# One core, same instructions: another order of the turns of an attention and MLP kernel

## The chip, the core and the metric

The kernel runs on one core of a Trainium2 chip. The metric is the device time of one execution in microseconds (us). The core has a matrix engine (PE in the profile, with its weight loads as PEld), VectorE (DVE), ScalarE (ACT), GpSimd (POOL), and a queue that only issues transfers (SP). Each executes its own list of instructions in order; semaphores make one wait for another. So the order in which the program issues instructions is the order in which each engine must take them.

## The reference

```
state = alpha[:, :, t, :, None] * state + einsum('bhd,bhe->bhde', k[:, :, t], v[:, :, t])
y[:, :, t] = einsum('bhd,bhde->bhe', q[:, :, t], state)          # for each t
x  = y with the heads side by side                                # (4, 768, 384)
xn = (x - mean) / sqrt(var + 1e-6) * g_ln
out = x + maximum(xn @ w_ch1, 0) @ w_ch2                          # 384 -> 1536 -> 384
```

Four batches of 8 heads, 768 steps and 48 channels go through a gated recurrence; its result goes through a normalisation and a two-layer MLP with a residual. The two weight matrices arrive as 64-bit floats.

## The kernel before

The 768 steps are cut into 6 chunks of 128. A chunk of one batch is one unit of attention, so there are 24 units, named a to x (a to d are chunk 0, e to h chunk 1, and so on). Within a chunk the recurrence is done by matrix products: logarithms of the gates are summed by a triangular matrix (L317, L320, L407), q and k are scaled by the exponentials (ACT L324 and L325, DVE L327 and L329), transposed (on PE, L355, in chunks 0 and 1; later on DVE, L366, and through DRAM on SP's queue, L372 and L379), multiplied into scores (L397, L405), masked by DVE (L411, L417), and turned into the result (L458, or L463 and L467). The state is carried by L432 on PE, L445 on DVE and a gate product on POOL (L447). Each result is copied out of PSUM (L493, L481), normalised (L512 to L523) and transposed (L530, or L536 and DRAM).

The MLP of chunk 0 is computed plainly: hidden products L567 (turns Y and Z, one per half of the batches), relu L570, second layer L579 (P and Q), residual L583. Chunks 1 to 5 use a scheme with fewer products: instead of nine block products it takes 15 of the first layer's (L857, turns 1 and 2 for the two halves of the hidden units) and 20 of the second layer's (L683, turn M), of combined blocks. Combinations are made by DVE: of the first weights (S), of the second weights (W, L643), of x (X, L834), of the hidden values after the relu (N, L670). Results are put together by DVE from PSUM (L867 to L900, L693, L696), by ACT (copies L865, L873, L887, L702 to L743) and by late adds on POOL (L876 to L896, L699). R and U are the relus (ACT L907), O fetches the residual.

The weights are brought in twelve pieces, turns A to L (A to F the first matrix, G to L the second). Each piece is loaded into one of three staging buffers and rounded from 64 bits to 32 by three DVE instructions (L219, L221, L223), one on ACT (L227) and further ones on DVE (L229 with L233 or L236). The load of the piece three later is issued in the last turn.

Six PSUM banks are shared by all products (tag "bank"). A product can start only when a bank has been read out by its last reader.

Every unit is a Python generator; each yield ends one turn. The order of all turns is written out by hand as one string of 1508 letters, and a letter executes the next turn of its generator:

```
turns = {"YZ"[h]: first_of_chunk_0(h) for h in range(2)}
turns |= {"PQ"[h]: second_of_chunk_0(h) for h in range(2)}
turns |= {chr(ord("a") + n): attention(n // B, n % B) for n in range(NCB * B)}
turns |= {chr(ord("A") + i): take_weights(i) for i in range(len(pieces))}
turns |= {"M": mlp(), "S": combine_first(), "W": combine_weights(),
          "1": hidden_products(0), "2": hidden_products(1), "R": relus(0), "U": relus(1),
          "X": (x for c in range(1, NCB) for x in combine_x(c)),
          "N": (x for c in range(1, NCB) for x in combine_hidden(c)), "O": outputs()}
with tc.manual_schedule():
    for turn in ORDER:
        next(turns[turn], None)
```

"Turn 17 of i" below means the code of unit i between its 17th and 18th yield, counted from 0. A turn issues between none and eight or so instructions; the products of one unit's turn 17 are 64 small matmuls.

Of the kernel before, what the change touches and what calls it, by code (L numbers as in the profile page):

```python
# [30 lines left out]


ORDER = (
    "bacabcadaacbcaadbcadabcababbebaccbadbaaBbccaedcbceAeeaaacbfecfBcdafddeaedbdeafae"
    "bcdccbfgadhAdcgCcdbebeebfhggdfgbfffbCdcgfgecdfchgdfhgabcddchdhAiiegjhacehedhhjfg"
    "biAdfidAeBhBijffYYiCjZZYYifZYlZCgjYDlYYjjZZYBZYgDieEgDgDjZZekEhZYGZgZigZGeeYgYgg"
    "fZYEhfGfkChihiYFYijfgEhgkhFZYhgYfghijgkFeZZlGZShfZYHlhHfYFYZeZHelYiZgllPmZkJIgJk"
    "PeiYjJIflHeSZIQgkIlYSjiPkffennSQlOKjLSnSjmSQhKnSjLnKPkiljnhSQnLkkjkWknkShOmPhkhl"
    "kOOhWlmmphmQmkmXjWQnXjlSQjPmkilXSXkP2OXWjXQjkjW2iXoSWX2oWX22Pi2mnol1j1mom2omSpoo"
    "l1XSpk2oW2m112p1m2pm11m1W211pp12O122r22jnn21lpnmnjSml1riOn2l12Rl111kqS1m21W1Rkp2"  # L40
    "o21mUXpq1mU2rUrnmj1rl2Rno2oomqonrormpokO1rNM2Mipin1op1ionoqUM2qp2W12RkMmNqiMoRtk"
    "UrpkqNM1NoMliMlNUMMNMNMKNqMlNorMWrnmtltNRMsqppMWNMriMMMpNlsqqqnoqttNttMtMsXMMssM"
    "sMNMNMX1oXXppMvstM2MXMMNMsppXoMXoqMsMMXM1nqqv11Xq1trMq2tqX21rn12v1r2ur2r222rvsqs"
    "svsu1rs1nuvvt2s11ss11p22rtsvosn2uropuXru222221uts212stnU1211u1121222Op1Rp2tRU21R"
    "Us1pXqU11x2tO2MM1vwMUM12xuRvu1vurNNNNwtOuuMwRxvNtxRNutwwMM2MOwNXwMNuXMMtNM1rMMMw"
    "qtXMMMxNUNxtMMsNMMMxXxMtXtrMMqMNrMXNvutMMwNuMMMNMMMxMLMOM11vvuq2X2O2wMus1wX11222"
    "2r2Xt1222w22utsqxvw2x2ww1vx21sX12121xwvq2O2x2w111u1uvU121w12s1wuRvx12U11J1q21R1U"
    "OvRxU121wMMu2xxsRNMw2NNMRM1MUNN2MMuUMqXN1MrNNRMNvMXNXMMMM2MMMxNM1uNXMMNMNMOXMXMv"
    "MMXOMMMXxNxwxMMvNMMMMMXMx21w1x222212v12w222x122w2212X11UX2212121121121wx111MU11X"
    "2RR2v1211212211R1URU211XOUM2XNRX1MX1RM2MXN2MXNXNMXXMXMMMN111U1MN1M1122MNM1MM2MM1"  # L50
    "11NNN121O11NM1MM21N1112N1122M1MMM12MM12N222M22M2RM1M2N22MM2MU1ON2M22M2UURR22RNNM"
    "MNM1MMOMRMNMUUM2ONMNNNMO2MMMUMNMMMMMRMMNNMMMNMNMMNMMMMMMMMNMNMMMMMMM"
)


# [913 lines left out]
```

## Time and profile before

| | |
|---|---|
| time, median of 3 runs | 420.37 us (420.18 to 420.57) |
| the profiled execution's own time | 420.64 us |
| its span, first to last instruction | 418.9 us |
| granted PE clock | 1.00 |
| bytes moved by DMA | 59.52 MB, 142 GB/s on average |

The span is the part that the profile covers; the rest of the profiled execution's time, 1.7 us, lies around it. Busy shares are of the span. An idle engine is listed with the instruction that waited and the one that released it. The chain that ended last is followed back from the last instruction, at each step to what released it.

### The profile page before, as it was taken

What the parts mean: (1) busy time and instruction counts of PE and PEld (TensorE: products, weight loads), DVE (VectorE), ACT (ScalarE), POOL (GpSimd) and SP (SyncE); (2) the same over time, 40 slices, a digit from 0 to 9 for tenths busy, and PEclk for the clock granted to TensorE, in tenths of its full rate; (3) what the DMA queues carried; (4) which work ended last, traced back from release to release, by engine and by line L of the source; (5) the groups of instructions that cost most, each with busy time, mean ns of one, the idle gap of its engine ahead of it and who ended that gap; (6) DMA issues with size and microseconds to landing.
All of it is one profiled execution on the core that took longest, in us unless ns stands there. A gap on an engine that the chain in (4) does not pass through costs nothing.

```text
span 418.9 us, 11553 instructions
## 1 busy us (share of the span) xinstructions
PE 409.0 (98%) x4608; PEld 360.9 (86%) x4608; DVE 351.4 (84%) x713; ACT 178.0 (42%) x440; POOL 153.2 (37%) x169
## 2 busy tenths in 40 slices
PE   6998999999999999999999999999999999999996
PEld 4787888766678889998889999889998899999996
DVE  3999999999999989996888996688876767977873
ACT  5498456724243496414546612364313242014110
POOL 3011000003203990043395033493152940499123
PEclk9999999999999999999999999999999999999999
DMA  7998889987778778587784546433035200001201
GB/s 247 325 297 246 206 201 293 287 194 181 145 221 176 200 167 185 128 195 178 146 215 70 130 105 166 88 95 77 0 114 104 67 1 2 0 20 38 94 20 56
DMA packets 133741, 59.52 MB, mean 142 GB/s; under 512 B 90764, under 2 KB 129804, under 8 KB 133688
## 3 DMA queue, kind: packets, MB, share of 16 engines
q1 hardware_dynamic: 133688, 58.79, 55.1%
q8 instruction: 36, 0.59, 0.6%
q14 instruction: 17, 0.14, 0.1%
HBM read 42.17 MB, written 16.61 MB: 140 GB/s over the span
## 4 chain that ended last, share of the span: by engine, by line
PE 89%; DVE 4%; ACT 2%; DMA 2%; issue 1%; SPq 1%; POOL 0%; POOLq 0%; DVEq 0%
PE hps L857 31%; PE ops L683 30%; PE ops L579 8%; PE hps L567 8%; PE aps L405 3%; PE yps L463 3%; PE yps L467 2%; PE sums L432 2%; DMA rq<-in_q_dram 2%; PE xps L530 1%; PE tps L355 1%; PE aps L397 1%; PE lps L407 1%; SPq L132 1%; DVE w L221 0%
## 5 line engine op out<-in xcount | busy, mean ns | idle before, releaser
L699 POOL TENSOR_TENSOR ob<-ob,u 128x192 f32<-128x192 f32 x40 | 26.3, 668 | 64.5 <-DVE ob L696 48.3
L857 PE MATMUL hps<-sum,w 128*128 128x256 f32 x192 | 46.3, 381 | 0.0
L907 ACT ACTIVATE hT<-hT 128x512 f32<-128x512 f32 x48 | 28.8, 624 | 34.9 <-POOL hT L879 18.5
L447 POOL TENSOR_TENSOR mid<-mid,gate 112x192 f32<-112x192 f32 x20 | 11.4, 568 | 80.0 <-DVE mid L445 33.3
L683 PE MATMUL ops<-w,hT 128*128 128x192 f32 x224 | 40.5, 327 | 0.0
L857 PEld LDWEIGHTS hps<-sum,w 128*128 128x128 f32 x192 | 36.1, 190 | 5.0
L683 PEld LDWEIGHTS ops<-w,hT 128*128 128x128 f32 x224 | 37.1, 190 | 0.7 <-issue 0.2
L857 PE MATMUL hps<-xT,w 128*128 128x256 f32 x136 | 34.0, 380 | 0.0
L579 PE MATMUL ops<-w,hT 128*128 128x384 f32 x96 | 33.0, 491 | 0.0
L567 PE MATMUL hps<-xT,w 128*128 128x256 f32 x144 | 32.5, 382 | 0.0
L567 PEld LDWEIGHTS hps<-xT,w 128*128 128x128 f32 x144 | 27.0, 190 | 4.2
L683 PE MATMUL ops<-ws,sum 128*128 128x192 f32 x160 | 28.7, 327 | 0.0
L857 PEld LDWEIGHTS hps<-xT,w 128*128 128x128 f32 x136 | 25.5, 190 | 3.1
L683 PEld LDWEIGHTS ops<-ws,sum 128*128 128x128 f32 x160 | 26.5, 190 | 0.3
L579 PEld LDWEIGHTS ops<-w,hT 128*128 128x128 f32 x96 | 17.6, 190 | 10.7 <-DVE w L236 0.3
L693 DVE TENSOR_TENSOR ob<-ops,ob 128x192 f32<-128x192 f32 x50 | 17.3, 353 | 10.6 <-PE ops L683 6.5
L447 POOL TENSOR_TENSOR st<-st,gate 112x192 f32<-112x192 f32 x16 | 11.7, 729 | 37.3 <-DVE st L445 25.9
L683 PE MATMUL ops<-ws,hT 128*128 128x192 f32 x128 | 23.6, 328 | 0.0
L463 PEld LDWEIGHTS yps<-st,qT 48*64 48x64 f32 x320 | 19.9, 134 | 4.0 <-issue 2.0
L467 PE MATMUL yps<-vx,at 64*64 64x48 f32 x320 | 22.7, 219 | 0.0
L463 PE MATMUL yps<-st,qT 48*64 48x48 f32 x320 | 22.0, 220 | 0.6 <-ACT x L493 0.6
L405 PEld LDWEIGHTS aps<-qT,kT 48*64 48x64 f32 x576 | 19.0, 134 | 4.1 <-issue 0.8
(255 smaller groups left out, 1134.2 us busy)
## 6 DMA issues: line engine op xcount, KB each, us to landing
ws<-in_moe_w_ch_dram SPq DMA_DIRECT2D x12, 768.0 KB, 5.9
td<-tr SPq DMA_DIRECT2D x64, 96.0 KB, 3.1
vn<-in_v_dram SPq DMA_DIRECT2D x12, 384.0 KB, 4.3
kept<-x SPq DMA_DIRECT2D x20, 192.0 KB, 3.0
ob<-kept SPq DMA_DIRECT2D x20, 192.0 KB, 3.1
out_dram<-ob SPq DMA_DIRECT2D x19, 192.0 KB, 1.9
ra<-in_alpha_dram SPq DMA_DIRECT2D x16, 192.0 KB, 2.6
kT<-td SPq DMA_DIRECT2D x32, 96.0 KB, 4.2
```

Of the source, the lines that this page charges most:

```text
L405: nc.tensor.matmul(to, kT[rs, p, s], qT[rs, p, s], start=True, stop=True)
L432: nc.tensor.matmul(up[h, p], qk_of(c, b)[ts, 1, p, i, :h.stop - h.start], vn[ts, i, p], start=True, stop=True)
L447: nc.gpsimd.tensor_mul(new, new, by)
L463: nc.tensor.matmul(yps[i][halves[s], i, p], qT[rs, p, s], (now, mid)[s][rs, p], start=True, stop=r != i)
L467: nc.tensor.matmul(yps[r][halves[s], i, p], at[halves[r], p, s], by, start=r != i, stop=True)
L567: nc.tensor.matmul(hps, w1[:, j // 2, f, j % 2 * P:][:, :P], xT_of[0][:, f, bs], start=(f == 0), stop=(f == NF - 1))
L579: nc.tensor.matmul(ops_of[b], hT_of[c][:, j, b], w2[:, j], start=(j == 0), stop=(j == NJ - 1))
L683: nc.tensor.matmul(acc, lhs[:, j], rhs[:, j], start=(j == 0), stop=(j == NT - 1))
L693: nc.vector.tensor_add(x, acc, x)
L699: getattr(nc.gpsimd, f"tensor_{op}")(x, x, y)
L857: nc.tensor.matmul(acc[:, i], w, b, start=True, stop=True)
L907: nc.scalar.activation(out=x, in_=x, func=AFT.Relu)
```

## The change

Only the string ORDER differs. The functions, the buffers, the transfers and the number of times that each letter occurs are the same. The new sequence was found by a search in which the durations on VectorE, ScalarE and GpSimd were drawn at random. The first three and the last two of its nineteen lines:

```diff
 ORDER = (
-    "bacabcadaacbcaadbcadabcababbebaccbadbaaBbccaedcbceAeeaaacbfecfBcdafddeaedbdeafae"
-    "bcdccbfgadhAdcgCcdbebeebfhggdfgbfffbCdcgfgecdfchgdfhgabcddchdhAiiegjhacehedhhjfg"
-    "biAdfidAeBhBijffYYiCjZZYYifZYlZCgjYDlYYjjZZYBZYgDieEgDgDjZZekEhZYGZgZigZGeeYgYgg"
...
-    "11NNN121O11NM1MM21N1112N1122M1MMM12MM12N222M22M2RM1M2N22MM2MU1ON2M22M2UURR22RNNM"
-    "MNM1MMOMRMNMUUM2ONMNNNMO2MMMUMNMMMMMRMMNNMMMNMNMMNMMMMMMMMNMNMMMMMMM"
+    "bOacaabccabacadadabcabababacbdbebabcaacbccdccaedbeefBAeeaacfcbcbfdaedBeddaeaebcf"
+    "fdcabAcdcgcdcecdeddChgeggbffbffabghfddfgcgaebCdcdhbdbgaghhfedaedibhAhgchhjhefCdB"
+    "cigfAkAdgilhBYZiZiBfjjZZiYfjliYjOjCYZZZZgefYgfjeYDggiZhDeZEYDhYZEgYZDYjeGkYigYZZ"
...
+    "NM111N12MMR1NMM2N1M121MMMM1NXRMNMM1N1M1NOMMMM2MM22222UNM22MRM2UM22OR221M1U2NM2MN"
+    "U2MR2M1NNM2OMUMM1MMNMNNMNNR2MMMNMMUMJMNMOMMMNMMNMNMMMMMMMNMMNMMMMMMM"
 )
```

The stretch of both strings in which chunk 0's second layer ends and the first products of the block scheme begin:

```diff
-...jlSQjPmkilXSXkP2OXWjXQjkjW2iXoSWX2oWX22Pi2mnol1j1mom2omSpool1XSpk2oW2m112p1m2pm...
+...WPPQXPSXiXpkiQojkQWSXjiXWSjX2kW2kpW222SollmXm21Wnjkiomjom1ool1o21S11mnplX2122m1op...
```

More of the change, by code (lines that the diff above doesn't have):

```diff
@@ L33 @@
 ORDER = (
-    "bacabcadaacbcaadbcadabcababbebaccbadbaaBbccaedcbceAeeaaacbfecfBcdafddeaedbdeafae"
-    "bcdccbfgadhAdcgCcdbebeebfhggdfgbfffbCdcgfgecdfchgdfhgabcddchdhAiiegjhacehedhhjfg"
-    "biAdfidAeBhBijffYYiCjZZYYifZYlZCgjYDlYYjjZZYBZYgDieEgDgDjZZekEhZYGZgZigZGeeYgYgg"
-    "fZYEhfGfkChihiYFYijfgEhgkhFZYhgYfghijgkFeZZlGZShfZYHlhHfYFYZeZHelYiZgllPmZkJIgJk"
-    "PeiYjJIflHeSZIQgkIlYSjiPkffennSQlOKjLSnSjmSQhKnSjLnKPkiljnhSQnLkkjkWknkShOmPhkhl"
-    "kOOhWlmmphmQmkmXjWQnXjlSQjPmkilXSXkP2OXWjXQjkjW2iXoSWX2oWX22Pi2mnol1j1mom2omSpoo"
@@ L40 @@
[L40 to L50, printed above, removed]
-    "11NNN121O11NM1MM21N1112N1122M1MMM12MM12N222M22M2RM1M2N22MM2MU1ON2M22M2UURR22RNNM"
@@ L52 @@
-    "MNM1MMOMRMNMUUM2ONMNNNMO2MMMUMNMMMMMRMMNNMMMNMNMMNMMMMMMMMNMNMMMMMMM"
+    "bOacaabccabacadadabcabababacbdbebabcaacbccdccaedbeefBAeeaacfcbcbfdaedBeddaeaebcf"
+    "fdcabAcdcgcdcecdeddChgeggbffbffabghfddfgcgaebCdcdhbdbgaghhfedaedibhAhgchhjhefCdB"
+    "cigfAkAdgilhBYZiZiBfjjZZiYfjliYjOjCYZZZZgefYgfjeYDggiZhDeZEYDhYZEgYZDYjeGkYigYZZ"
+    "GEghfiChejgEfgkfYFYOgghYjgFfhkYiZGhZfkZfFSZlYggjZefYfYiYYZkihHFekYllHliZnnlZGHIh"
+    "imgSlgmHhfYIZiIJSfPeejZPYSeJQeKlkQISljJPSjhQlSKKnhQPnknnLjLhjkShnmjLSSkkikPnlkWk"
@@ new lines @@
+    "khlWmmhmmhXOXmWPPQXPSXiXpkiQojkQWSXjiXWSjX2kW2kpW222SollmXm21Wnjkiomjom1ool1o21S"
+    "11mnplX2122m1op1mpn1m2m1j22nWpp112222OpnlQnl2Sllmmn2Sj112q1jpR12r12U1jm11X1oR121"
+    "lnUjir2m2pl1pRrWmrOln2okroUiorponn2iroroq1noq21oMlp1oMkOMqqWlqMR1MqRNpq1NUUikMlN"
+    "MO2NorMqMMMsimiNNpMWNMMMkk2MWNMtppormNRUotMMrMqnkoqqqNtpnrNMnttttLtXMNMpssm2smMN"
+    "nXMpsMqMNstMNsMMMoNXM1mXXXsXMpMMsvqMMMXM1X112n22q1vqtrqM12p12tqq22r2rvXvo2uro2r1"
+    "1srsssvvvvs1ur1strs12121tpsuOutsp21p1Ou21u2qu2R2121pss122111Xo222tn2pU11UuR22w21"
@@ new lines @@
+    "U1RM2vu2oxMMUs21MNuvtutwUrnONvNuxNwRuqsttORtwq1MMNwtMMtqM1tuXMMNNRMMUMXMNNvNMuxK"
+    "NMsrtMNMwxswMwXMxMMMqNMMMXXMwvuMNvqxMXMxNMxMOMNuMMuXMMt1XM212X21rv22x2w1Ms22222t"
+    "21wwswq2svxxX22v11xXU1212w21v11sw211111111rR22urt11r1122xRUwR1q1vUN2O2v2MOOw1xxv"
+    "12rMuU1NMNMMrMw2RUNRN1tXNw2MNMRMUNMXNNMuMMMvNwXvMXwMx2MMNMMMMONxwMMMuNX1MuuXMMMX"
+    "MxNMxMNMuxMMMMMM1w2xXvw2112XOxM2Xx221w122x21211X1222112x21121U2112vR11122w1222x2"
+    "2X11Uu221vRU1121X1U21RXXX2X2MXNMMMNU1MNX12RR1R2XOM1NMN11N11U2MO211M12NM11M21MX1M"
```

## The prediction

> **What bounds the kernel now.** I read the page first, then the idle time by engine pair, the stretches of 15 us, the chain that ended last, and the timeline where they disagreed.
>
> ```profile
> span 418.9 us, 11553 instructions
> ...
> PE 409.0 (98%) x4608; PEld 360.9 (86%) x4608; DVE 351.4 (84%) x713; ACT 178.0 (42%) x440; POOL 153.2 (37%) x169
> ...
> PE 89%; DVE 4%; ACT 2%; DMA 2%; issue 1%; SPq 1%; POOL 0%; POOLq 0%; DVEq 0%
> ```
>
> The matrix engine (PE) is busy 409.0 of 418.9 us, and 89% of the chain that ended last runs on it. Busy alone proves little, since matmul ends are modelled, so I checked the steps between starts. They are even: eight records of L683 take 1.30 us and four of L857 0.86 us all through the chain, which is 0.163 and 0.216 us each. The clock row is 9 in every slice. From 40 us to 415 us PE is therefore fed; what is not matmul lies at the ends and in a few waits.
>
> ```profile
> PE lps L317 <- ACT la L312: 2.4, 1, 2.4
> PE xps L530 <- DVE xn L519: 1.6, 1, 1.6
> PE lps L254 <- DVE more L251: 1.1, 1, 1.1
> PE yps L463 <- ACT x L493: 0.6, 1, 0.6
> ```
>
> These are all its idle stretches of 0.5 us or more. The first three belong to the first 35 us. Only the fourth lies in the main part (at 115 us; by starts of records it is 0.83 us). The stretches show the second engine:
>
> ```profile
> 30.00:45.00 15.00, 13.13 (x221) 11.24 (x213) 14.86 (x32) 12.13 (x31) 2.76 (x5) 1.00 0.88 251
> 75.00:90.00 15.00, 15.00 (x59) 10.11 (x58) 14.76 (x24) 7.92 (x18) 0.51 (x1) 1.00 0.89 249
> 165.00:180.00 15.00, 15.00 (x241) 14.31 (x240) 14.32 (x33) 6.68 (x18) 1.81 (x3) 1.00 0.62 147
> 195.00:210.00 15.00, 15.00 (x281) 13.04 (x280) 11.59 (x28) 7.79 (x22) 4.64 (x7) 1.00 0.68 154
> ```
>
> The columns after the stretch and its length are PE, weight load, DVE (VectorE), ACT, POOL. Up to 180 us DVE is as full as PE (14.3 to 14.9 of 15); after that it has a fifth to spare. So in the first 180 us two engines are full at once and feed each other; afterwards PE alone sets the pace.
>
> **What the change moves.** Counting the letters: both strings have 1508 turns and each letter equally often, so every engine executes the same instructions; only the order in each queue differs. No instruction has a price of its own. The cost is the sum of four terms.
>
> (1) *Small tiles between large ones.* Attention products use 64-row tiles, the rest 128-row ones, and going back costs time:
>
> ```profile
> 76.39 2.58 PE ops L579 x8
> ...
> 103.68 2.78 PE ops L579 x8
> 106.79 0.50 PE sums L432 x32
> 107.29 2.78 PE ops L579 x8
> ```
>
> The same eight records take 2.58 us behind other large matmuls and 2.78 us behind a small group: 0.20 us, and with the gaps at entry and exit in the timeline up to 0.33 us per excursion. Reading the PE instructions off the strings, the order changes between small and large 66 times before and 62 after: two excursions fewer, 0.4 to 0.7 us of PE time. All four changes lie in the first 180 us.
>
> (2) *The wait at 115 us.* Before, two attention results (k and i, turn 17, L463) stand behind each other while accumulators of the second layer hold banks; the second waits until ACT has read a bank (L493, 115.08 to 115.57). In the new string three stand in a row (i, j, k), but with two of chunk 0's results already added and their banks free (P's turns 5 and 7 on DVE are ahead of them), and 1.1 us of another result between i's and k's bank. I expect this wait to go: 0.83 us of PE time. A wait of 0.35 us at 36.3 us (L432 for the state add L445) goes too, since the next scores now stand ahead of it.
>
> (3) *Start.* The first hidden product (L567) starts at 39.69 us, 0.01 us after VectorE finished weight piece A (L233). In the new DVE order the four instructions that finish A stand in the same places, behind the same instructions, only permuted; so it starts at the same 39.7 us, plus or minus 0.5. PE has done 0.7 us less by then (a transposition and a score group moved behind it). That is a loss of 0.7 us against (1) and (2). On DVE's and ACT's side nothing is gained: the normalisations of chunk 0 (L519) that PE waited for (1.6 us at 33 us) are permuted, with b's now last instead of c's; PE reaches that point with 1.1 us more work still to do and 0.9 us earlier, which is even to 0.2 us.
>
> (4) *What is late next.* Here the freed time must pass DVE. For places where PE needs a DVE result I added, in each string, the PE work ahead (steps between starts in the trace) and the DVE work ahead (durations less overlap), and took from the trace when DVE had done that much. The difference "time DVE gets there minus PE work ahead" is how much PE must have lost by that point:
>
> - before: 7.85 at the first hidden product, 9.0 at chunk 0's last third (piece L, PE work 95), 9.0 at the sums of l (98), 9.9 at the scores of p (136), 11.4 at the 19th product of layer 2 (176), 12.3 at the 25th hidden product of the first half (201). What PE had really lost there: 7.9, 9.0, 9.1, 10.3, 11.6, 12.4. So the margins are 0.0 to 0.4 us.
> - after: 8.55 at the same start, 9.5 at the second third (pieces I and J, PE work 82), 9.8 at the sums of l (97), 10.1 at m's result (127), 11.65 at the 19th product (175), 13.4 at the 26th hidden product of the second half (200).
>
> Until 176 us of PE work both orders owe DVE nearly the same (11.65 against the 11.6 lost); what (1) and (2) free on PE, 1.2 to 1.5 us, PE spends waiting for weight pieces and state adds instead (0.5 to 0.7 us more at 82 and 97). I book (1) to (3) together at 0 and keep minus 1.5 as their end. The last item asks 1.0 us more than before lost (13.4 against 12.4). It takes DVE to be as late as in the trace of before, but after 180 us DVE waits for PE part of the time, so its lateness is partly PE's own. Between 0 and 1.0 I take 0.3, nearest to the row of 195 to 210 us, where DVE has 3.4 of 15 us free.
>
> *ACT, POOL and DMA.* ACT is 42% busy; the shortest way from a relu (L907) to the combination that reads it is 0 to 1.3 us of PE work in both strings, ten times before and nine after. POOL's late adds stand as near to their readers as before (2.6 us the nearest in both). On SP's queue the transpose by DRAM (L366 to the scores L405) has 11.2 us of PE work at the least before, 11.9 after; page section 6 gives 3.1 us to write and 4.2 us to read back. Some read-backs now stand directly ahead of their scores in the string (k, m), but SP has run ahead by then: what stands in front of them in its queue is ready 5 us earlier. Cost nothing; if SP were held there, up to 4.2 us once.
>
> One pair of rows shows engines disturbing each other: the first pass over weight piece A (L219) took 1.18 us beside a POOL memset, the other eleven a median of 0.55, and a gate product on POOL (L447) took 2.44 us at 96 us where 0.51 is usual. The Trainium skill, "GPSIMD Engine Reference", section "1. Specifications", says that GpSimd's SBUF interfaces are shared with VectorE and contend with two-port and two-input instructions; the rows agree. By that rule the new order, which puts A's first pass ahead of the memset, could start 0.6 us earlier, and the sum would be 420.1 instead of 420.7; I leave it out of the sum, since other pairs move together elsewhere.
>
> *The end.* The last combination (L670) stands seven products ahead of the end in both strings, and the output instructions behind them are the same: nothing.
>
> Sum: 0 from (1) to (3), plus 0.3 from (4), against the profiled run's own time of 420.64 us (span 418.9) and the median of 420.37, which is 0.27 lower. From the median: 420.7 us.
>
> **Rivals.**
> *A, the forecast:* both engines full, debts equal; 419.6 to 421.2. Chance 0.42.
> *B, PE's savings reach the end:* if DVE has in truth more slack than the sums say (it idles 0.1 to 1.1 us in each 15 before 180 us, partly for PE), the 0.4 to 0.7, the 0.83 and part of the 0.35 us stay: 420.37 less 1.2 to 1.9, 418.5 to 419.2. For it: DVE's own waits on score products (L417 on L405, 3.9 us in total). Against it: weight piece L was ready 0.04 us before its product. Chance 0.27.
> *C, slower by a wait for a bank at 200 us of PE work:* the 26th hidden product of the second half needs the bank that DVE frees with the first half's turn 47. If DVE comes there as late as in the trace, PE waits the full 1.0 us, and the same lateness shows again at piece J (0.5): 421.4 to 421.9. It decides from the point where DVE's share of that stretch is over about 13 of 15. For it: hidden products of both halves alternate there, so each bank is read later. Against it: 11.59 of 15. If the read-backs of k or m are also held on SP, 422.5. Chance 0.31.
>
> **How the numbers follow.** About 0.2% (0.84 us) is what a measurement of this kernel can tell from no change. Faster is B, 0.27; within is A, 0.42; slower is C, 0.31. The range reaches from inside B to C's end without the held queue: 418.7 to 422.2. A's own range is 419.6 to 421.2.
>
> **What would show it.** Steps between starts of L683 and L857 unchanged, and PE busy within 1 us of 409 (basis). No wait of L463 on L493 (2). First L567 at 39.2 to 40.2 us (3). New short waits of PE on DVE at weight piece J near 92 us and at the sums of l near 107 us (4). A wait of a second-half hidden product near 213 us decides between A and C. DVE still at 14.3 or more of 15 from 75 to 180 us is A; 13.8 or less with PE ahead is B. I am wrong as a whole if a wait on a DMA or on POOL stands among PE's waits.

## The result, and the profile after

The changed kernel takes **423.31 us** (median of 13 runs, 422.66 to 426.85) where the kernel before takes 420.3 us in the 13 runs beside it: a ratio of 1.0074, 95% interval 1.0047 to 1.01. It is slower by 3 us, and 1.1 us above the end of the predicted range. Two further series of the changed kernel gave 424.62 and 424.22 us, with 420.55 and 420.76 us for the kernel before. The profiled run of each of these two is the lowest of its series (423.02 and 423.09 us), so the profiles account for 2.4 to 2.7 us above the profiled run of before (420.64 us); what makes the medians of these series 1.1 to 1.6 us longer than their profiled runs is in no profile.

```profile
span 421.6 us, 11558 instructions
...
PE 410.7 (97%) x4608; PEld 361.5 (86%) x4608; DVE 350.5 (83%) x713; ACT 178.0 (42%) x440; POOL 152.0 (36%) x169
...
PE 81%; DMA 7%; DVE 6%; SPq 3%; issue 1%; ACT 1%; DVEq 0%; ACTq 0%
```

Every engine does the same work as before (PE 410.7 against 409.0 us, DVE 350.5 against 351.4), in a span 2.7 us longer. The chain that ended last now lies on PE for 81%, not 89%; 7% of it are transfers. The list of PE's waits says where (instruction that waited, releaser, us in all, times, longest):

```profile
...
PE aps L405 <- DVE w L221: 0.7, 1, 0.7
PE yps L463 <- ACT x L493: 0.6, 1, 0.6
PE hps L857 <- ACT xT L532: 0.6, 1, 0.6
PE yps L467 <- ACT x L493: 0.5, 1, 0.5
PE ops L683 <- DVE u L894: 0.4, 1, 0.4
PE ops L683 <- DVE sum L670: 0.4, 1, 0.4
```

The lines left out belong to the first 35 us. Of these six, only the kind of the second stood in the list of before. They lie at 64, 114, 215, 116, 155 and 170 us. The stretches that were shown of before:

```profile
30.00:45.00 15.00, 13.62 (x217) 11.66 (x210) 14.86 (x30) 12.15 (x31) 1.48 (x3) 1.00 0.96 271
75.00:90.00 15.00, 15.00 (x74) 10.40 (x67) 14.72 (x26) 7.64 (x17) 0.51 (x1) 1.00 1.03 239
165.00:180.00 15.00, 14.63 (x235) 13.47 (x235) 13.57 (x31) 10.17 (x29) 0.51 (x1) 1.00 0.62 154
195.00:210.00 15.00, 15.00 (x380) 13.17 (x377) 11.81 (x31) 7.65 (x23) 4.47 (x7) 1.00 0.55 126
```

VectorE (third number) is as full as before up to 90 us and has 1.4 of 15 us free at 165 us, where it had 0.7. It is not the engine that became later.

**PE's loss.** To place the 3 us I compared the start of each PE group with the bare PE work ahead of it: the steps between starts, for each pair of neighbouring kinds the lower quartile of what the trace of before shows, added up along each kernel's own order (399.8 us before, 399.7 after). The difference grows only where PE loses time. Its growth, in us, between points of equal PE work (add 8 to 17 us for the time in the trace):

| PE work | to 31 | 31–64 | 64–97 | 97–119 | 119–161 | 161–203 | 203–end | sum |
|---|---|---|---|---|---|---|---|---|
| before | 7.83 | 0.69 | 0.56 | 1.15 | 1.10 | 1.07 | 2.01 | 14.41 |
| changed | 7.33 | 1.84 | 0.65 | 1.91 | 2.02 | 1.75 | 1.83 | 17.33 |
| changed, 2nd profile | 6.95 | 2.23 | 0.65 | 1.90 | 2.01 | 1.75 | 1.55 | 17.04 |
| changed, 3rd profile | 6.59 | 2.13 | 0.64 | 1.91 | 2.04 | 1.75 | 2.04 | 17.10 |

The profiled times are 406.0 to 406.2 us plus the sum. From 64 to 203 us of work the three profiles of the changed kernel agree to a few hundredths of a us. So the 2.6 to 2.9 us in the sums are: 1.2 to 1.5 us at 31–64 us of work, 0.76 at 97–119, 0.92 at 119–161, 0.68 at 161–203, less 0.5 to 1.2 us gained in the start.

Three of the places, in the timeline (start, duration, engine, operation, and in brackets the idle time before it and its releaser). The scores of j:

```profile
64.31 0.61 PE L405 MATMUL aps<-qT,kT 48*64 48x64 f32 x3 [0.71 <-DVE w L221]
```

The releaser named is wrong here: the bank that these scores take had been read at 61.8 us. The built program lets L405 wait for the read-backs of q and k too, and their semaphores came at 64.18 and 64.55 us. The second and third profile name them; in the second:

```profile
PE aps L405 <- DMA qT<-td: 1.2, 1, 1.2
```

SP issued these four read-backs at 56.37 to 58.93 us; before at 59.48 to 61.06 us. The last is issued 2.1 us earlier and lands 2.55 us earlier (64.55 instead of 67.10), but j's scores had moved 4.6 us forward (from 60.2 to 55.6 us of PE work). Before, they came at 68.50 us, 1.4 us behind the last landing. The wait is for a straggler: each read-back raises its semaphore in sixteen steps; of the last one, fifteen were in by 63.29 us and the sixteenth came at 64.55 (before 65.45 and 67.10).

The three results in a row:

```profile
114.09 0.49 ACT L493 ACTIVATE x<-yps 128x384 f32<-128x384 f32 x1 [5.40 <-PE yps L463]
114.63 0.25 PE L463 MATMUL yps<-st,qT 48*64 48x48 f32 x1 [0.64 <-ACT x L493]
115.88 0.49 ACT L493 ACTIVATE x<-yps 128x384 f32<-128x384 f32 x1 [0.89 <-PE yps L467]
116.42 0.25 PE L467 MATMUL yps<-vx,at 64*64 64x48 f32 x1 [0.55 <-ACT x L493]
```

Both times PE writes into a bank that ACT has only just read: j's result follows i's into i's first bank, k's second half follows j's into j's first bank. By starts PE loses 0.82 and 0.81 us. And at 215 us:

```profile
213.97 0.49 PE L530 MATMUL xps<-consts,xn 128*128 128x128 f32 x3
214.50 0.48 ACT L532 COPY xT<-xps 128x384 f32<-128x384 f32 x1 [1.26 <-PE xps L530]
215.03 1.13 PE L857 MATMUL hps<-sum,w 128*128 128x256 f32 x4 [0.57 <-ACT xT L532]
```

The product L857 takes the very bank that the transposition directly ahead of it on PE had filled, so it waits for PE's own result, ACT's copy of it and the semaphore: 0.73 us.

### The profile page after: what moved, and what is told of

It is laid out like the page before. It is cut to its first block, busy times and chain, and to the rows that moved or that the text cites. A ratio compares the mean times of both kernels' runs of the same rounds, so it can differ in the third digit from the quotient of the medians.

```text
span 421.6 us, 11558 instructions
## 1 busy us (share of the span) xinstructions
PE 410.7 (97%) x4608; PEld 361.5 (86%) x4608; DVE 350.5 (83%) x713; ACT 178.0 (42%) x440; POOL 152.0 (36%) x169
## 4 chain that ended last, share of the span: by engine, by line
PE 81%; DMA 7%; DVE 6%; SPq 3%; issue 1%; ACT 1%; DVEq 0%; ACTq 0%
PE hps L857 31%; PE ops L683 31%; PE ops L579 7%; DMA ws<-in_moe_w_ch_dram 5%; PE hps L567 3%; PE aps L405 3%; PE yps L463 2%; PE yps L467 2%; DMA vn<-in_v_dram 2%; PE sums L432 2%; PE xps L530 1%; SPq L372 1%; SPq L132 1%; DVE w L233 1%; DVE w L221 1%
## 5 line engine op out<-in xcount | busy, mean ns | idle before, releaser
L699 POOL TENSOR_TENSOR ob<-ob,u 128x192 f32<-128x192 f32 x40 | 27.2, 690 | 58.8 <-DVE ob L696 43.0
L857 PE MATMUL hps<-sum,w 128*128 128x256 f32 x192 | 46.7, 382 | 0.6 <-ACT xT L532 0.6
L857 PEld LDWEIGHTS hps<-sum,w 128*128 128x128 f32 x192 | 35.9, 190 | 5.6 <-ACT xT L532 0.8
L683 PE MATMUL ops<-w,hT 128*128 128x192 f32 x224 | 40.2, 327 | 0.4 <-DVE u L894 0.4
L683 PEld LDWEIGHTS ops<-w,hT 128*128 128x128 f32 x224 | 37.3, 190 | 1.3 <-ACT few L522 0.8
L857 PE MATMUL hps<-xT,w 128*128 128x256 f32 x136 | 34.3, 383 | 0.1
L567 PE MATMUL hps<-xT,w 128*128 128x256 f32 x144 | 32.8, 384 | 0.0
L579 PE MATMUL ops<-w,hT 128*128 128x384 f32 x96 | 32.3, 489 | 0.0
L567 PEld LDWEIGHTS hps<-xT,w 128*128 128x128 f32 x144 | 26.8, 190 | 4.1 <-DVE qk L327 0.4
L683 PE MATMUL ops<-ws,sum 128*128 128x192 f32 x160 | 28.7, 327 | 0.4 <-DVE sum L670 0.4
L857 PEld LDWEIGHTS hps<-xT,w 128*128 128x128 f32 x136 | 25.3, 190 | 3.5 <-issue 0.4
L579 PEld LDWEIGHTS ops<-w,hT 128*128 128x128 f32 x96 | 17.8, 190 | 11.3
L683 PEld LDWEIGHTS ops<-ws,sum 128*128 128x128 f32 x160 | 26.4, 190 | 0.9 <-DVE sum L670 0.6
L405 PEld LDWEIGHTS aps<-qT,kT 48*64 48x64 f32 x576 | 19.0, 134 | 6.4 <-issue 1.6
L683 PE MATMUL ops<-ws,hT 128*128 128x192 f32 x128 | 23.7, 329 | 0.0
L405 PE MATMUL aps<-qT,kT 48*64 48x64 f32 x576 | 22.0, 222 | 1.7 <-ACT kT L360 0.9
L447 POOL TENSOR_TENSOR st<-st,gate 112x192 f32<-112x192 f32 x16 | 9.4, 589 | 36.8 <-DVE st L445 36.8
L467 PE MATMUL yps<-vn,at 64*64 64x48 f32 x320 | 22.3, 219 | 0.0
```

What stands on the lines that cost most here:

```text
L405: nc.tensor.matmul(to, kT[rs, p, s], qT[rs, p, s], start=True, stop=True)
L447: nc.gpsimd.tensor_mul(new, new, by)
L467: nc.tensor.matmul(yps[r][halves[s], i, p], at[halves[r], p, s], by, start=r != i, stop=True)
L567: nc.tensor.matmul(hps, w1[:, j // 2, f, j % 2 * P:][:, :P], xT_of[0][:, f, bs], start=(f == 0), stop=(f == NF - 1))
L579: nc.tensor.matmul(ops_of[b], hT_of[c][:, j, b], w2[:, j], start=(j == 0), stop=(j == NJ - 1))
L683: nc.tensor.matmul(acc, lhs[:, j], rhs[:, j], start=(j == 0), stop=(j == NT - 1))
```

## The experiments

The theory: PE alone sets the end, and each wait that a place of the string makes for PE costs its length, there and nowhere else. The rivals: VectorE is owed the time in any case (a wait undone comes back at the next place), or the waits are chance. Each kernel is the changed one (or the one before) with other turns; letters of the string are shown.

| kernel | median us (runs) | lowest | before, beside it |
|---|---|---|---|
| scores_later | 423.35 (8) | 422.15 | 420.56 |
| results_apart | 423.83 (6) | 423.25 | 420.56 |
| new_then_old | 421.69 (12) | 420.78 | 420.56 |
| old_then_new | 423.78 (6) | 422.12 | 420.56 |
| changed_again | 424.62 (6) | 423.02 | 420.55 |
| three_undone | 421.66 (12) | 420.02 | 420.55 |
| undone_and_i_later | 422.69 (12) | 421.02 | 420.55 |
| old_two_moved | 421.19 (12) | 420.03 | 420.55 |
| old_i_with_m | 424.13 (6) | 422.54 | 420.36 |
| undone_k_with_m | 421.36 (11) | 420.16 | 420.36 |
| changed_third | 424.22 (10) | 423.09 | 420.76 |
| scores_later_again | 424.33 (9) | 423.05 | 420.76 |
| banks_undone | 423.30 (9) | 421.26 | 420.53 |
| three_undone_again | 422.10 (12) | 420.62 | 420.53 |

PE's loss by stretch:

| kernel | to 31 | 31–64 | 64–97 | 97–119 | 119–161 | 161–203 | 203–end | sum |
|---|---|---|---|---|---|---|---|---|
| scores_later | 7.27 | 0.69 | 0.95 | 1.90 | 2.00 | 1.76 | 1.55 | 16.12 |
| scores_later_again | 7.52 | 1.61 | 1.29 | 1.90 | 3.26 | 1.75 | 1.43 | 18.76 |
| results_apart | 7.27 | 4.79 | 0.65 | 0.34 | 2.67 | 3.31 | 1.45 | 20.48 |
| banks_undone | 7.31 | 3.15 | 0.65 | 0.34 | 2.14 | 1.06 | 1.89 | 16.54 |
| three_undone | 6.98 | 1.75 | 0.65 | 0.34 | 2.13 | 1.06 | 1.76 | 14.67 |
| three_undone_again | 7.26 | 0.70 | 1.18 | 0.34 | 3.70 | 1.06 | 1.83 | 16.07 |
| new_then_old | 7.16 | 1.79 | 0.65 | 1.90 | 1.68 | 1.07 | 2.01 | 16.26 |
| old_then_new | 7.48 | 0.69 | 0.56 | 1.15 | 2.04 | 1.90 | 1.62 | 15.44 |
| old_two_moved | 7.29 | 1.70 | 0.56 | 0.41 | 1.49 | 1.10 | 2.14 | 14.69 |
| old_i_with_m | 9.18 | 1.82 | 0.87 | 0.75 | 4.59 | 1.11 | 2.01 | 20.33 |

Where the results are parted (results_apart, banks_undone, three_undone), the profiled time is 406.5 us plus the sum, not 406.0: the bare work holds 0.5 us for two more excursions. So of what the sum gains there, 0.5 us has to be taken off.

### The two halves: new_then_old, old_then_new

```
ORDER = first 496 turns of one string + the other string without the turns already done
```

> The first 496 turns of the changed kernel, the remaining 1012 turns in the sequence of the kernel before (turns already done are left out, so nothing is issued twice); the seam is at about 120 us. Theory (each wait is local to its place in the string and adds up): PE's loss is that of the changed kernel up to the seam (1.5 us more than before) and that of the kernel before behind it: 421.8, between 421.3 and 422.3. Rival (lateness of VectorE is carried along, so that PE time lost early is not lost again later): the short waits of the kernel before at 154 us (0.33) and 265 us (0.56) are absorbed, 420.9 to 421.2.

> The first 496 turns of the kernel before, the remaining turns in the sequence of the changed kernel; the seam is at about 120 us. Theory (local and additive): PE loses nothing more than before up to the seam and what the changed kernel adds behind it (1.4 us: the waits at 155, 170, 215 and 232 us less the kernel before's at 154 and 265): 421.7, between 421.2 and 422.2. Rival (debt to VectorE: without the early losses the later waits grow by as much): 423.0 to 423.5, with a wait over 1.2 us at the product that waited 0.73 us at 215 us.

By their profiles both follow the theory. Behind the seam old_then_new loses 5.56 us, the changed kernel 5.60, although PE comes there 1.85 us earlier (9.88 against 11.73 us lost). Its waits are those of the changed kernel:

```profile
PE yps L463 <- ACT x L493: 0.6, 1, 0.6
PE hps L857 <- ACT xT L532: 0.6, 1, 0.6
PE ops L683 <- DVE u L894: 0.4, 1, 0.4
PE ops L683 <- DVE sum L670: 0.4, 1, 0.4
```

The first of these is the one of the old order at 115 us, the rest are the new ones. If PE owed that time to VectorE, coming earlier would have lengthened them. new_then_old has the changed kernel's 1.90 us at 97–119 and before's 1.07 at 161–203. Its median, 421.69, is as expected; that of old_then_new (423.78) lies above what either side had expected, and its profiled run (422.12) is its lowest, so its half is shown by the profile alone.

### The scores of j: scores_later, scores_later_again

```diff
-...ghYjgFfhkYiZGhZfkZfF...
+...ghYgFfhkYiZGhZfkZjfF...
```

> The changed kernel with one turn moved: turn 9 of j (its scores L405) stands two hidden products (L567, 2.6 us of PE work) later in the string, so that PE no longer reaches it before SP's read-backs of j's transposed q and k have landed. Theory (PE alone is full, each of its waits costs its length at the end): the wait of 0.78 + 0.37 us at 64 us is gone, the PE work from 70 us on runs 0.9 to 1.2 us earlier than in the changed kernel, and the time falls by the same, from 423.3 to 422.1 to 422.5. Rival (VectorE is as full as PE up to 180 us, and PE must wait for it in any case): the wait at 64 us goes, but the waits at 92 to 117 us or at 155 to 170 us grow by as much, and the time stays at 423.3 within 0.3.

> The changed kernel with turn 9 of j two hidden products later, once more. Its first profile showed PE 1.2 us less behind from 64 us to the end, its first median (423.35) hardly any gain. Theory (the wait at 64 us costs its length, and the first median lay high by chance, or on a chip on which the changed kernel lies higher too): 0.8 to 1.6 us less than the changed kernel beside it. Rival (what PE gains at 64 us it loses elsewhere in most executions): within 0.4 us of it.

> The changed kernel, nothing edited, beside the next one on one chip, since the first run of the kernel with j's later scores had no run of the changed kernel beside it. Median 423.2 to 424.7, as in its two runs so far (423.31, 424.62).

In the first profile the wait is gone and PE is 1.2 us less behind to the end. The medians do not follow: 423.35, then 424.33 beside 424.22 for the changed kernel. Here the theory failed as I had put it. The second profile shows 1.61 us lost at 31–64 us of work all the same: PE stood still within the 64 products of g's result, directly ahead of i's scores, and went on 0.65 us later, at 59.76 us. Three other profiles have such a step at the same place, of 0.73 to 0.99 us (three_undone, undone_k_with_m, new_then_old), and none has a releaser for it:

```profile
PE yps L467 <- issue: 0.4, 1, 0.4
```

I had put it down to i's scores waiting for their own read-backs. In three of the four the last read-back of i landed 0.06 to 0.13 us before PE went on, but in new_then_old it landed at 58.38 us, 1.4 us before. So this cause is not shown; what is shown is that a kernel loses this time in one execution and not in another (scores_later has no such step), and that it can come with j's scores unmoved (new_then_old).

### The results: results_apart

```diff
-...XiXpkiQojkQWSXjiXWSjX2kW2...
+...XiXpkiQoQjWSXjiXWSjX2kkW2...
```

> The changed kernel with two turns moved: the three attention results i, j, k (turn 17) that stood in a row are parted, by Q's turn 6 (four products L579) between i and j and by the first product of the block scheme (L857) with other turns between j and k. Theory (two results in a row need four banks; the second takes a bank that ACT still has to read, and PE waits for that copy L493): the waits of 0.82 and 0.81 us at 114 and 117 us go, two more excursions to small tiles cost up to 0.33 us each, and the time falls by 0.9 to 1.4 us, from 423.3 to 421.9 to 422.4. Rival (the banks are short because VectorE is late with its share of the reading, not because of the place): a wait of 0.5 us or more at the parted results or at the first L857 remains, and the time is within 0.5 us of 423.3.

The two waits went: 0.34 us is lost at 97–119 instead of 1.91. The time did not fall in this series. Its profile lost 2.4 us at the read-backs of j (the string is that of the changed kernel there) and 1.7 us more as PE's granted clock fell behind them (last section); and 3.31 us instead of 1.75 at 161–203, with two waits of 0.70 and 0.54 us that have no releaser (at 200 and 208 us). These two are in no profile of the next kernels, which have the same turns moved. The figure of this place was taken again in the next kernels.

### Both and p's transposition: three_undone, banks_undone

```diff
-...u2R2121pss122...
+...u2pR2121ss122...
```

> The changed kernel once more, nothing edited, beside the next three on one chip. Theory (the waits belong to places of the string): the profile shows the same waits of PE at 114, 117, 155, 170, 215 and 232 us with the same lengths within 0.1 us, and at 64 us a wait for the read-backs that may differ between executions (0.78 + 0.37 us in the first profile; 0.70 + 1.74 us in the profile of the kernel with the parted results, whose string is the same up to there), median 423.3 to 424.0. Rival (the waits are chance, from durations that differ between executions): two or more of the six are gone or at other places.

> The changed kernel with four turns moved: the scores of j (turn 9) two hidden products later; Q's turn 6 between the results i and j, and k's result behind the first L857; p's turn 25 (transposition L530, at 214 us) five turns and three products earlier, so that the product that took its bank no longer stands directly behind it. Theory (each wait local, each undone separately): 1.2 us at 64 us, 1.6 us less 0.3 to 0.7 for the added excursions at 114 to 117 us, and 0.7 us at 215 us are gained; PE's loss against its bare work falls from 17.3 to 14.4 to 15.0 us and the time from 423.3 to 420.4 to 421.0. Rival (the banks are handed out anew behind every moved turn, and as many new waits come as old ones go, like 0.80 and 0.78 us at 200 and 208 us in the kernel with the parted results): 421.8 to 422.8.

The six waits named there came again at the same places, 0.23 instead of 0.50 us at 231 us, the others within 0.04; the median of the changed kernel, 424.62, is above what was expected. With three places undone the time falls by 3.0 us on the same chip (424.62 to 421.66; the lowest runs 423.02 and 420.02). The sum, 14.67, is as the theory had it; the median lies between its range (to 421.0) and the rival's (from 421.8). The list of PE's waits has lost all lines on ACT x and ACT xT:

```profile
...
PE yps L467 <- issue: 0.7, 1, 0.7
PE ops L683 <- DVE u L894: 0.4, 1, 0.4
PE ops L683 <- DVE sum L670: 0.4, 1, 0.4
```

Next the banks alone (the results and p's transposition moved, j's scores not):

> The changed kernel with only the two places undone at which PE waited for a bank (results i, j, k parted; p's transposition earlier); the scores of j stand where the change put them. Theory (the time is lost at the banks; what PE waits for read-backs at 60 to 64 us differs between executions and is only partly given back by a later j): PE's loss between 97 and 119 us of work 0.2 to 0.4 instead of 1.85, between 161 and 203 us 1.0 to 1.1 instead of 1.9, time 2.0 to 2.6 us below the changed kernel's 423.3 to 424.6: 421.2 to 422.4. Rival (the read-backs matter as much as the banks): 1.0 us or more above the kernel with all three undone beside it.

> The kernel with three places undone (scores of j later, results parted, p's transposition earlier) beside the one that leaves j's scores where they are. Theory: 0 to 0.8 us below it. Rival: 1.0 us or more below it.

The two bank places gain 1.57 and 0.69 us in each of the three profiles, 2.26 in all, of which the added excursions take 0.5. The median of banks_undone is 423.30, above what was expected, and 1.2 us above three_undone_again, whose loss at j's scores is gone: the read-backs matter too, as the rival said, though with 9 and 12 runs that spread over 4.9 and 3.7 us. In the profile of banks_undone PE waits 2.03 us for them, longer than in any profile of the changed kernel:

```profile
65.60 0.62 PE L405 MATMUL aps<-qT,kT 48*64 48x64 f32 x3 [2.03 <-DMA qT<-td]
```

### i later as well, and k beside m: undone_and_i_later, undone_k_with_m

```diff
-...ghfiChejgEfgkfYFY...
+...ghfChejgEfgfYikFY...
```

> As the kernel before it (three places undone), and the scores of i (turn 9, with turn 2 of k, which reads what they prepare) one hidden product later, 1.3 us of PE work, since in one profile they waited 1.00 us for their own read-backs. Theory (the read-backs of i and j are late by amounts that differ between executions, and that is what spreads the times of the changed kernel over 2 us and more): the lowest run is within 0.5 us of that of the kernel before it, and the runs lie closer together, the upper quarter within 1 us of the median. Rival (the spread has another cause): lowest and highest run as in the kernel before it, within 0.4 us.

The lowest run is 1.0 us higher than that of three_undone, the upper quarter begins 0.9 us above the median instead of 1.6: neither theory is borne out clearly. The profile has 0.55 us lost at j's scores again, and two waits with no releaser, 0.27 us at 153 and 0.99 us at 159 us.

```diff
-...QoQjWSXjiXWSjX2kkW2kpW222SollmXm21W...
+...QoQjWSXjiXWSjX2W2pW222SollmXkmk2k1W...
```

> The changed kernel with three places undone as before (scores of j later, results apart, p's transposition earlier), but with k's result (turns 17 to 19) beside the scores of m, so that one excursion to small tiles less is added. Theory: as the kernel with three places undone, less 0.3 us: PE's loss at the end 14.3 to 14.8, 420.1 to 421.4. Rival: k's sums come later to VectorE, and its later results, or new waits for banks, cost 0.5 us or more: 421.7 to 422.5.

421.36 against 420.36 us of before beside it, with a sum of 14.75 us, as expected. It does not beat the kernel before.

### The old order without its wait: old_two_moved, old_i_with_m

```diff
-...jPmkilXSXkP2OXWjX...sqxvw2x2ww...
+...jPmklXSXkPi2OXWjX...sqw2xvx2ww...
```

> The kernel before with two places changed: i's result (turn 17) behind P's turn 6 (four products L579, 2.6 us) instead of directly behind k's result, and the scores of x (turn 9) with the result of v (turn 15) one L857 product later at 264 us. Theory (a wait of PE for a bank costs its length at the end in the old sequence as in the new one): the waits of 0.80 us at 115 us and 0.56 us at 265 us go, one excursion to small tiles more costs 0.3 us, and the time is 419.2 to 419.7, faster than both kernels. Rival (PE then meets VectorE's results earlier and waits there): waits of 0.3 us or more appear between 120 and 180 us, and the time is 420.1 to 420.6.

The wait at 115 us went (0.41 us lost instead of 1.15), but 0.4 us more is lost at 119–161, the order has one excursion more, and 1.0 us more is lost at 31–64, where the string is that of before: PE waits there for a load of v (L432 for DMA vn, 0.8 us), which the profile of before doesn't have. The 0.56 us at v's result came again, and neither profile lists a wait there: the scores ahead of it issue more products than those that my step lengths came from, so I had taken work for a wait. No gain: 421.19 (lowest 420.03) against 420.55 (419.94).

```diff
-...PmkilXSXkP2OXWjXQjkjW2iXoSWX2oWX22Pi2mnol1j...
+...PmklXSXkP2OXWjXQjkjW2XoSWX2oWX22P2iminoil1j...
```

> The kernel before with three turns moved: i's result (turn 17) no longer directly behind k's but three products of the block scheme later, beside the scores of m, so that no excursion to small tiles is added; its copy and sum (turns 18, 19) follow it. Theory (PE's wait for the bank that ACT reads costs its length, and nothing is paid for parting the two): the wait of 0.80 us at 115 us goes with no excursion in exchange; PE's loss between 97 and 119 us of work falls from 1.15 to 0.3 to 0.5, and the time is 419.5 to 419.9 against 420.3 to 420.5 of before on the same chip. Rival (the banks are handed out anew behind the move, and new waits take as much): a new wait of 0.4 us or more between 120 and 160 us, time equal to before within 0.3 us.

Both expectations missed this one: new waits came, as the rival said, but the time is 424.13 us, 3.8 us above before. The wait at 115 us is gone, and PE loses 4.59 us at 119–161 instead of 1.10. (The profiled run took 426.55 us, since more was lost at other places too: 1.4 us in the start, where PE's clock fell, as the last section shows, and 1.1 us at 31–64.) SP's queue shows why; first before, then this kernel:

```profile
118.01 0.45 SPq L554 DMA_DIRECT2D ob<-kept  x1
118.56 0.40 SPq L138 DMA_DIRECT2D vn<-in_v_dram  x1
...
126.47 3.16 SPq L372 DMA_DIRECT2D td<-tr  x4
```

```profile
120.58 0.43 SPq L554 DMA_DIRECT2D ob<-kept  x1
124.34 0.40 SPq L138 DMA_DIRECT2D vn<-in_v_dram  x1
...
132.39 2.90 SPq L372 DMA_DIRECT2D td<-tr  x4
```

The load of the next v values needs the buffer that i's result reads, and SP's list of waits says so:

```profile
SPq L138 <- PE yps L467: 3.3, 1, 3.3
```

With i's result later, SP stood still from 121.0 to 124.34 us, and all that is queued behind the load, the writes of transposed q and k among it, came 5.9 us later, where this execution as a whole was only 2.6 us behind. VectorE's next transposition had to wait for those writes:

```profile
137.47 0.98 DVE L366 STREAM_TRANSPOSE tr<-qk 128x768 f32<-128x768 f32 x1 [1.57 <-DMA td<-tr]
```

VectorE is busy 7.92 of the 10 us from 130 us on, and PE stands still five times for 0.29 to 0.66 us between 139 and 160 us, four of them until VectorE is done.

## Why the prediction was wrong

*What bounds the kernel* was right: PE, step by step; the places of loss are PE's waits, and L683 and L857 kept 0.163 and 0.216 us per step.

*(1) Excursions, 0.4 to 0.7 us.* Not found. Bare work differs by 0.1 us, PE's busy time rose by 1.7. In both traces PE leaves the large products (L567, L579, L857, L683) for attention products and comes back 25 times; so the two excursions that were counted as saved are not among those whose price was read off.

*(2) "I expect this wait to go: 0.83 us of PE time."* **The first step that failed.** The small wait at 36.3 us went, but this one did not; there are two, 0.82 and 0.81 us. I had argued from the string which banks were free (P's turns 5 and 7 ahead). The string gives only the order; which bank a product takes is chosen when the program is built, and it gave j the bank that i had just filled. Undone, the place is worth 1.57 us, about 1.0 after the two excursions that parting the results adds.

*(3) Start.* First L567 at 38.46 us, not 39.7: VectorE had the first half of piece A ready 1.2 us earlier. Worth 0.5 to 1.2 us by 31 us of work. The rule that was left out of the sum did bear on it: the first pass over A now began 0.15 us ahead of the memset and took 0.56 us; this time the memset beside it was the longer one, 1.30 instead of 0.95 us. That agrees with the interfaces shared between GpSimd and VectorE of the Trainium skill, "GPSIMD Engine Reference", section "1. Specifications". The pass is 0.6 us shorter than before, half of the 1.2 us; the other half was not followed up.

*(4) The debts to VectorE.* The bank wait at the 26th hidden product of the second half is there, as rival C had it, 0.73 us where I took 0.3 of 0 to 1.0. But it is not a debt: ACT's copy releases it, not VectorE's turn 47, and in old_then_new it has the same length with PE 1.85 us earlier. The account of lateness through VectorE sent me to the right place for the wrong reason; that a wait came there was luck. It also booked (1) to (3) at 0 because VectorE would take them back at pieces I and J and the sums of l; no such wait is in the list. The two waits on VectorE in the main part, 0.4 us each, are at 155 and 170 us.

*ACT, POOL and DMA, "Cost nothing".* **The second step that failed.** I compared the PE work between L366 and L405 as a minimum over all units (11.2 and 11.9 us) and so missed that j's scores had moved 4.6 us forward, while their read-backs landed only 2.55 us earlier, with 1.4 us to spare before. I had also priced the way by the page's 3.1 and 4.2 us; for j it takes 17.1 us from L366 (47.47 us) to the last landing, 16.8 before. Cost: 1.2 to 1.5 us, and 2.5 us in banks_undone. The last sentence of the prediction named this sign.

The direction was rival C's, but only its bank wait of 0.7 us is in the 3 us; the read-backs held were j's, not k's or m's, and the wait at the results had been booked as a gain. The range was too narrow since three places failed together, where I had one. **Open:** the 0.92 us at 119–161. Of it 0.54 is M's turn 0, which waits for a bank that VectorE (L894) reads at 153.75 to 154.4 us; no run moved it. The 0.54 us at 170 us (L683 waiting for N, L670) was also left as it is, and stands in all kernels with the new second part.

## What to carry to other kernels

Where one engine is fed without a gap, a new order of the same work can be judged place by place: look for every result that is followed at once by a product that needs a bank, and ask what reads that bank and when, in the built program and not in the listing. Compare each transfer with its own consumer, unit by unit; a minimum over all units hides the one that moved. And a result moved later also holds the buffers that it reads: the load waiting for them can stop a whole queue.

## What the runs showed of the hardware

**PE's clock can fall to half behind a short idle time.** In results_apart PE was idle for 2.08 of the 2.4 us before 65.9 us. Rows of that stretch (start and end, length, busy PE, PEld, DVE, ACT, POOL, granted clock, DMA share, GB/s):

```profile
63.00:66.00 3.00, 0.92 (x10) 0.43 (x12) 2.93 (x6) 1.48 (x4) 0.51 (x1) 1.00 0.96 336
66.00:67.00 1.00, 1.00 (x35) 0.93 (x34) 1.00 (x2) 0.25 (x1) 0.00 (x0) 1.00 1.09 375
67.00:70.00 3.00, 3.00 (x9) 2.35 (x9) 2.93 (x6) 0.24 (x1) 0.00 (x0) 0.52 0.94 201
70.00:71.00 1.00, 1.00 (x5) 0.85 (x4) 1.00 (x4) 0.94 (x4) 0.00 (x0) 0.73 0.69 179
71.00:72.00 1.00, 1.00 (x7) 0.87 (x6) 1.00 (x3) 0.48 (x2) 0.00 (x0) 1.00 1.00 399
```

About a microsecond after PE had work again, its clock went to half for 3.4 us: eight steps of L567 took 0.427 us instead of 0.216, 1.7 us in all. The one other fall in the midst of work, in the sixteen profiles, is in old_i_with_m: PE was idle for 2.00 us up to 8.91 us, and the clock was at half from 9.64 us, for as long:

```profile
9.64:13.05 3.41, 3.41 (x13) 2.66 (x12) 1.77 (x5) 2.31 (x5) 0.00 (x0) 0.50 1.07 372
```

Idle time as long does not always do it: 2.03 us at the first place in banks_undone, 2.36 us at the second in the kernel before and 2.61 in old_then_new left the clock at 1.00. That the idle time is the cause is likely from the order of events, and not tested. The Trainium skill, "TensorE: Matmul & The Clock Gate", section "Why this matters for your kernels", asks for no idle gaps over about 3 us, and its Part 1 says that the window in which activity is judged is free-running. That equal gaps end differently fits such a window. The 3 us are too generous for these two profiles, where gaps of 2.0 and 2.1 us were followed by a fall. A loss of 1.7 us fits the mean clock of 0.996 of the runs of the changed kernel at 426.55 and 426.85 us, about half of what they are above their median.

**PE waits that nothing explains.** In eight of the sixteen profiles PE stood still once or twice for 0.3 to 1.3 us with no releaser, mostly within the 64 small matmuls of one result; four times at the result of g near 59.5 us and three times at that of o near 158 us. What it waited for was not tried. The executions of one kernel spread over 2 us and more; these waits, the read-backs and the clock are parts of that, but how large each is was not measured. So the stretches carry the verdicts here, and the medians only where they differ by more.
